# Order of steps in a float64-to-float32 weight conversion, and of GpSimd's block sums, in a fused attention and Fourier-MLP kernel

## The chip, the cores and the metric

The kernel runs on one core of one Trainium2 chip. The metric is the device time of one execution in microseconds (us). A core has five engines with a queue of instructions each: TensorE (PE in the profile, with its weight loads as PEld), VectorE (DVE), ScalarE (ACT), GpSimd (POOL) and SyncE (SP), which here issues most of the DMA transfers. An engine takes its own queue in order; between engines, an instruction waits for the instruction whose data or buffer it needs.

## The reference

Chunked attention gives x; a Fourier mixing and an MLP with layer norm follow:

```python
scores = scale * np.matmul(q_c, k_c.transpose(0, 1, 2, 4, 3))   # 8 batches, 8 heads, 9 chunks of 64, D 64
attn = np.exp(scores - max); attn = attn / (sum + 1e-09)
x = np.matmul(attn, v_c)                                        # bridged to (8, 576, 512)
u = x + np.real(fft(fft(x, axis=1), axis=2))
un = (u - mu) / np.sqrt(var + 1e-06)
out = u + np.maximum(un @ w_ch1, 0.0) @ w_ch2                   # w_ch1 512x2048, w_ch2 2048x512
```

The two weight matrices arrive as float64. VectorE and ScalarE have to turn every weight into float32 from its two 32-bit halves before TensorE can use it.

## The kernel before

The work goes through nine groups of token tiles (`groups`), each with an up product (`w1`), a Relu and a down product (`w2`). Group 0 runs plainly (`up_first`, then `down_plain`), group 1 has a plain up product and a down product in half-sized blocks, and the later groups use half-sized blocks for both, whose sums and differences of weight blocks are stored in device memory once (`keep1`, `keep2`, both on GpSimd). The code is under a manual schedule: the order of the calls in the Python program is the order in each engine's queue.

The main loop (lines 1315 to 1352) takes one step of `mlp(g)` at a time and counts it in `t`. Group 0 has KF = 16 up steps (`t` 1 to 16: four blocks `f` of four output tiles, four steps `kk` each) and 16 down steps (`t` 17 to 32: one row block m of `w2` each, four matmuls). On every fourth up step the block is complete and ScalarE writes four Relus (line 1065), which read the PSUM tiles that the next block needs. Behind each step of the MLP the body of the loop puts, in this order: the next steps of the attention and Fourier work of the next batch (`sides`: transposes, scores, softmax, `att_V`, folding, then `fourier`), then weight pieces (`round_next`), then up to three steps of the sums for `keep2` (line 1337).

**A weight piece.** There are 32 pieces of 128x512 weights: 0 to 15 are `w1`, 16 to 31 `w2`; down step m needs piece 16 + m. The raw halves land by DMA in one of seven spaces (`spaces`), from piece 26 on in three only; a piece's load can start once the piece before it in that space is read out. `round_weight(i)` puts the first half of piece i ("h") and then the second half of piece i - 1 ("t") into the queues:

- VectorE 322: fraction bits (AND), into the place of the weight; ScalarE 314: turned into a float between 1 and 2.
- VectorE 325: exponent bits (AND), into `power`; ScalarE 317 and 320: two Relus that make a power of two of them.
- for piece i - 1, VectorE 335: the low half is added to the fraction (waits for 314); 336: the sign is set on the power (waits for 320); 337: fraction times power. Line 341 then issues the next load.

The steps `t` = 1 to 16 call `round_next` five times in four steps (twice at `t` = 4, 8, 12), so pieces 7, 12, 17 and 22 are those begun at `t` = 3, 7, 11 and 15, the steps ahead of the Relus. Piece 0 is converted on its own in `attention_early`, ahead of the copies of `fourier_early` (lines 846 to 856), and the first half of piece 1 lies behind these (line 857, its ScalarE steps put off by hand).

**The joining.** `fourier(1)` sends its second products at `t` = 23 (`z_sets`, line 669). ScalarE copies four short rows (`z_middle`, 708) and two half tiles (`z_odd`, 694), VectorE joins them (`z_joined`, 699 and 703), ScalarE spreads the result (732 to 735 into `zr`, then `zf`), and TensorE can run the first mixing product (`mix`, 788). The rows `y` (793) are combined on VectorE (798, 799) and added to x by VectorE and, for the mirrored tiles, GpSimd (805); mean and variance (652, 653) and the normalized rows `un` (942) follow, which TensorE transposes (347) for group 1.

**The sums of `keep2`.** Each of four rounds has four GpSimd operations (line 1017), an operand of which is the `w2` that VectorE has finished, and seven stores. They write into spaces that raw pieces have used. `n_sum < 5` lets the first four sums and their stores in once piece 26 is begun, the others once all pieces are done.

Of the kernel before, what the change touches and what calls it, by code (L numbers as in the profile page):

```python
# [8 lines left out]
FP32 = mybir.dt.float32  # L9
U32 = mybir.dt.uint32  # L10
ACTF = mybir.ActivationFunctionType
ALU = mybir.AluOpType
# [4 lines left out]
def kernel(  # L17
# [32 lines left out]
    nc = tc.nc  # L50
# [10 lines left out]
    KF = DFF // 128  # L61
# [84 lines left out]
    N_LATE, N_EARLY, N_LAST = 5, 8, 26  # L146
# [108 lines left out]
    def load_tables():  # L255

        token_tables(early_tk)
        for i in range(2):
            nc.sync.dma_start(out=first_rest[32 + 32 * i:33 + 32 * i, 0:DM], in_=dim_tab[0:1, 1 + 2 * i, :])
# [10 lines left out]
    def turn_dim_tables():  # L270
# [9 lines left out]
    pieces = [  # L280
        (w1[:, kk, f:f + 512], w_ch1[kk * 128:(kk + 1) * 128, f:f + 512])
        for f in range(0, DFF, 512)
        for kk in range(KD)
    ] + [(w2[:, m, :], w_ch2[m * 128:(m + 1) * 128, :]) for m in range(KF)]

    power = {}
# [3 lines left out]
    def raw(i):  # L290
        return spaces[raws[i]].bitcast(U32).rearrange("p (f r) -> p f r", r=2)

    def load_weight(i):

        fit = [r for r in free if (i < N_EARLY or r < N_LATE) and (i < N_LAST or r > 1)]
        if i < len(pieces) and fit:
            raws[i] = fit[0]
            free.remove(fit[0])
            nc.sync.dma_start(out=raw(i).rearrange("p f r -> p (f r)"), in_=pieces[i][1].bitcast(U32))

    def round_weight(i, later=None, parts="ht"):

        if "h" in parts and i < len(pieces):
            w, t = pieces[i][0], raw(i)
            lo, hi, wi = t[:, :, 0], t[:, :, 1], w.bitcast(U32)  # L310
            p = power[i] = three_p.tile([128, 512], U32, tag="o", name="power")

            def fraction(w=w, wi=wi):
                nc.scalar.activation(out=w, in_=wi, func=ACTF.Copy, scale=2.0 ** -20, bias=1.0)

            def exponent(p=p):
                nc.scalar.activation(out=p, in_=p, func=ACTF.Relu, scale=-1.0, bias=top[:, 0:1])

            def power_(p=p):
                nc.scalar.activation(out=p, in_=p, func=ACTF.Relu, scale=-8.0, bias=top[:, 1:2])  # L320

            nc.vector.tensor_scalar(wi, hi, 0x000FFFFF, None, ALU.bitwise_and)
            if later is None:
                fraction()
            nc.vector.tensor_scalar(p, hi, 0x7FF00000, None, ALU.bitwise_and)
            if later is None:
                exponent()
                power_()
            else:
                later += [fraction, exponent, power_]  # L330
        if "t" in parts and 0 < i <= len(pieces):
            w, t = pieces[i - 1][0], raw(i - 1)
            lo, hi = t[:, :, 0], t[:, :, 1]
            p = power.pop(i - 1)
            nc.vector.scalar_tensor_tensor(w, lo, 2.0 ** -52, w, ALU.mult, ALU.add)
            nc.vector.scalar_tensor_tensor(p, hi, 0x80000000, p, ALU.bitwise_and, ALU.bitwise_or)
            nc.vector.tensor_tensor(out=w, in0=w, in1=p.bitcast(FP32), op=ALU.mult)
            r = raws.pop(i - 1)
            if i - 1 + len(spaces) < N_EARLY or r < N_LATE:
                free.append(r)  # L340
            load_weight(max(raws, default=i - 1) + 1)
# [694 lines left out]
    lo, hi = slice(0, 256), slice(256, 512)  # L1036
# [203 lines left out]
    with tc.manual_schedule():  # L1240
        nc.vector.memset(warm, 0.0)
        make_identity(nc, ident)
        nc.vector.memset(eps, 1e-6)
        for r in range(4):
            nc.vector.memset(sign[32 * r:32 * r + 32], 2.0 * (r % 2) - 1.0)
        nc.vector.memset(top[:, 0:1], float((896 + 255) << 20))
        nc.vector.memset(top[:, 1:2], float(255 << 23))
        nc.scalar.preload_act_table_set("natural_log_exp_and_others")
        first_rest = three_p.tile([128, XW], FP32, tag="y", name="first_rest")
        for t in more_v + v_ring:  # L1250
            nc.vector.memset(t[:, :, :, D:DV], 1.0)
        for n in range(first[1]):
            load(n)
            if n < 3:
                load_v(n)
        load_v(3)
        load_v(4)
        load_tables()
        load_weight(0)
        load_dim_tables()  # L1260
        for i in range(1, len(spaces)):
            load_weight(i)
        n_w = 2
        idle = [ps_f.tile([128, 512], FP32, tag="ff", name="idle")]
        early_xp = [ps_f.tile([128, 512], FP32, tag="ff", name="early_xp") for _ in range(2)], None

        def keep_warm(times):

            for _ in range(times):
                nc.tensor.matmul(out=idle[0][:, 0:NQ], lhsT=warm[:, 0:128], rhs=warm[:, 0:NQ], start=True, stop=True)  # L1270

        put_off, first_ups = [], []

        def round_next(later=None):
            nonlocal n_w
            if n_w <= len(pieces):
                round_weight(n_w, later)
                n_w += 1

        keep_warm(8)  # L1280
        attention_early()
        turn_dim_row()
        for step, _ in enumerate(fourier_early()):
            if step == 0:
                turn_dim_tables()
        round_next()
        PAUSE = 3

        def side(b):
            yield from attention(b)  # L1290
            for _ in range(PAUSE if b == 1 else PAUSE - 1):
                yield
            yield from fourier(b)

        sides = [list_ for list_ in (side(b) for b in range(1, B))]
        sizes = []
        for b in range(1, B):
            n_tiles = first[b + 1] - first[b]
            sizes.append((4 * n_tiles + 1 if b == 1 else 3 * n_tiles + 1) + PAUSE + 2 + (b == 1) + NM + b % 2)
        done, cur = 0, 0  # L1300
        begin = [0]
        for g in range(NG):
            begin.append(begin[-1] + (KF if g < first_of[1] else 2 * HF) + (KF if g < first_of[2] else 2 * NO))
        ready_at = [begin[g] + (2 * KF - 7 if g < first_of[2] else 2 * HF + 4) for g in range(NG)]
        conv2 = iter([step for i in range(HF // 2) for step in [keep2(i)]])
        conv1 = iter([step for i in range(4) for step in [keep1(i)]])

        def chain(gens):
            for gen in gens:
                yield from gen  # L1310

        n_sum = 0
        conv2, conv1 = chain(conv2), chain(conv1)
        t = 0
        for g in range(NG):
            for _ in mlp(g):
                t += 1
                heavy = False
                if t == 8:
                    nc.scalar.copy(tk, early_tk[:, :, :, 0:NE])  # L1320
                if cur < len(sides):
                    t0 = 3 if cur == 0 else ready_at[cur - 1]
                    t1 = ready_at[cur]
                    due = min(sizes[cur], (t - t0) * sizes[cur] // (t1 - t0))
                    while done < due:
                        heavy = next(sides[cur], None) or heavy
                        done += 1
                    if t >= t1:
                        for _ in sides[cur]:
                            pass  # L1330
                        cur, done = cur + 1, 0
                if not heavy:
                    round_next()
                    if t <= 2 or t < KF and t % 4 == 0 or t >= KF + 3:
                        round_next()

                for _ in range(3):
                    if n_w > len(pieces) or n_w > N_LAST and n_sum < 5:
                        next(conv2, None)
                        n_sum += 1  # L1340
                if t == begin[1] - 1:
                    for _ in conv2:
                        pass
                if begin[1] <= t < begin[1] + KF // 2:
                    for _ in range(3):
                        next(conv1, None)
                if t == begin[1] + KF // 2:
                    for _ in range(NS2):
                        fetch(2)
                if t == begin[1] + KF:  # L1350
                    for _ in range(NS1):
                        fetch(1)
# [49 lines left out]
```

## Time and profile before

| | us |
|---|---|
| median of 3 runs (lowest, highest) | 1082.01 (1081.83, 1082.57) |
| the profiled execution: its time, and its span from first to last instruction | 1083.94, 1082.2 |
| TensorE busy in matmuls, share of the span | 1057.6, 98% |
| VectorE, ScalarE, GpSimd busy | 586.8, 309.4, 328.6 |
| TensorE idle that another engine ends, from 50 to 200 us | 1.1 + 2.6 + 4.4 + 0.5 + 0.4 |

From 240 us on TensorE is busy without a gap in almost every stretch of 20 us (in two of them it is 1.8 and 0.8 us short) until the last stretch; the idle time lies before, in the stage in which the weights are converted. There VectorE is busy 18 to 19.7 us of every 20 from 40 to 140 us, ScalarE 16 to 18 of every 20 from 40 to 100 us.

How to read the lines of the profile: a wait line has the engine and line that waited, what ended the wait, then the total, the number of times and the longest in us. A line of the timeline has the start, the time in us, engine, line, operation, and the tile written <- the tiles read; in square brackets stands the idle time of the engine just before it. In the chain of waits, a line has the start, the time and the engine and line that the end of the program hung on at that moment. In the table by stretches, each engine has its busy time and count, then come the clock granted to TensorE (1.00 is full speed), the share of the DMA engines' time, and GB/s.

### The profile page before, as it was taken

The numbers are of one execution on the slowest core, as the hardware profiler recorded it, in microseconds if no ns is written. First come the engines' busy times: TensorE is split into PE (matmuls) and PEld (weight loads), VectorE is DVE, ScalarE is ACT, GpSimd is POOL, SyncE is SP. The second block draws the span as 40 slices with busy tenths as digits, with TensorE's granted clock in tenths as the row PEclk, the third lists the DMA queues.
The fourth block names the chain that finished last, engine by engine and source line by source line (L and its number), as shares of the span: only waits on it lengthen the run. The fifth ranks groups of instructions, "written<-read, shape, count | busy, mean of one in ns | idle before, by whom it ended". The sixth has DMA issues, their size and how long they took to land.

```text
span 1082.2 us, 19747 instructions
## 1 busy us (share of the span) xinstructions
PE 1057.6 (98%) x7410; PEld 841.1 (78%) x7410; DVE 586.8 (54%) x1271; ACT 309.4 (29%) x730; POOL 328.6 (30%) x475
## 2 busy tenths in 40 slices
PE   8999989999999999999999999999999999999998
PEld 6645445446888888788888888888888888888887
DVE  4899986325556555664555555735664534323411
ACT  4788463222113320232122311331134103101300
POOL 4301026384513350163215331525151401310140
PEclk9999989999999999999999999999999999999999
DMA  8766555598557635793578356854663355346232
GB/s 176 237 196 180 153 175 199 143 292 275 192 172 229 198 118 173 222 266 105 168 214 252 112 176 179 253 174 150 184 199 104 144 173 177 123 151 213 78 117 78
DMA packets 147948, 192.65 MB, mean 178 GB/s; under 512 B 66284, under 2 KB 104172, under 8 KB 140686
## 3 DMA queue, kind: packets, MB, share of 16 engines
q1 hardware_dynamic: 144204, 187.98, 57.1%
q10 hardware_dynamic: 3330, 2.76, 1.0%
q8 instruction: 59, 0.97, 0.3%
q0 software_dynamic: 320, 0.66, 0.3%
q14 instruction: 35, 0.29, 0.1%
HBM read 167.22 MB, written 24.12 MB: 177 GB/s over the span
## 4 chain that ended last, share of the span: by engine, by line
PE 81%; DVE 6%; DMA 6%; ACT 4%; SPq 2%; issue 1%; POOL 1%; DVEq 0%; ACTq 0%; POOLq 0%
PE pb L1190 21%; PE pa L1141 17%; PE pa L1190 15%; PE pb L1141 13%; PE pt L347 3%; PE up L1074 2%; PE dn L1095 2%; PE mix L788 2%; PE z L669 1%; PE sc L398 1%; PE xp L448 1%; PE up L1054 1%; DMA v<-in_v_dram 1%; DMA out_dram<-o 1%; DMA q<-in_q_dram 1%
## 5 line engine op out<-in xcount | busy, mean ns | idle before, releaser
L1141 PE MATMUL pa<-unT,wa 128*128 128x256 f32 x672 | 159.9, 381 | 2.5 <-DVE wa L1149 2.5
L1141 PEld LDWEIGHTS pa<-unT,wa 128*128 128x128 f32 x672 | 126.3, 190 | 20.3 <-DVE wa L1149 3.0
L1042 POOL TENSOR_TENSOR h<-h 128x256 f32<-128x256 f32 x64 | 55.2, 870 | 232.6 <-DVE wb L1040 140.1
L1190 PE MATMUL pa<-wb,h 128*128 128x256 f32 x512 | 115.7, 380 | 0.0
L1190 PE MATMUL pb<-wb,h 128*128 128x256 f32 x512 | 114.9, 379 | 0.0
L1141 PE MATMUL pb<-wa 128*128 128x256 f32 x448 | 106.6, 381 | 0.0
L1190 PEld LDWEIGHTS pa<-wb,h 128*128 128x128 f32 x512 | 96.1, 190 | 12.9
L1190 PEld LDWEIGHTS pb<-wb,h 128*128 128x128 f32 x512 | 96.3, 190 | 12.6
L1141 PEld LDWEIGHTS pb<-wa 128*128 128x128 f32 x448 | 84.3, 190 | 11.5
L1095 PE MATMUL dn<-wb,h 128*128 128x512 f32 x128 | 60.8, 625 | 2.6 <-ACT h L1065 2.6
L505 POOL COPY xall<-xall 1x512 f32<-1x512 f32 x28 | 17.3, 617 | 149.7 <-DVE xall L465 120.4
L1147 DVE TENSOR_TENSOR wa<-pb,wa 128x256 f32<-128x256 f32 x56 | 23.8, 424 | 69.7 <-ACT wa L1146 69.7
L1190 PE MATMUL pb<-wb,yall 128*128 128x256 f32 x256 | 58.2, 381 | 0.0
L1190 PE MATMUL pb<-wb 128*128 128x256 f32 x256 | 57.7, 379 | 0.0
L1190 PE MATMUL pa<-wb,yall 128*128 128x256 f32 x256 | 57.6, 379 | 0.0
L1074 PE MATMUL up<-unT,wa 128*128 128x512 f32 x128 | 56.8, 596 | 0.0
L1146 ACT COPY wa<-pa 128x256 f32<-128x256 f32 x56 | 20.8, 372 | 123.8 <-PE pa L1141 81.0
L1141 PE MATMUL pa<-wa 128*128 128x256 f32 x224 | 53.9, 383 | 0.0
L1141 PE MATMUL pb<-unT,wa 128*128 128x256 f32 x224 | 53.0, 380 | 0.0
L1190 PEld LDWEIGHTS pa<-wb,yall 128*128 128x128 f32 x256 | 48.0, 190 | 6.1
L1190 PEld LDWEIGHTS pb<-wb,yall 128*128 128x128 f32 x256 | 47.7, 190 | 6.3
L1190 PEld LDWEIGHTS pb<-wb 128*128 128x128 f32 x256 | 47.7, 190 | 5.9
(265 smaller groups left out, 1770.0 us busy)
## 6 DMA issues: line engine op xcount, KB each, us to landing
wb<-s SPq DMA_DIRECT2D x56, 1024.0 KB
wa<-s SPq DMA_DIRECT2D x196, 256.0 KB
xall<-in_moe_w_ch_dram SPq DMA_DIRECT2D x22, 512.0 KB
q<-in_q_dram SPq DMA_DIRECT2D x96, 112.0 KB
k<-in_k_dram SPq DMA_DIRECT2D x96, 112.0 KB
v<-in_v_dram SPq DMA_DIRECT2D x124, 64.0 KB
yall<-in_moe_w_ch_dram SPq DMA_DIRECT2D x10, 512.0 KB
s<-wb SPq DMA_DIRECT2D x20, 256.0 KB
```

The source lines that it names most:

```text
L347: nc.tensor.transpose(pt[:, j, :], src(j), ident)
L398: nc.tensor.matmul(out=sc[t0:t0 + CH, e, j * CH:(j + 1) * CH], lhsT=a[r0:r0 + D, 2 * j + c, 0:CH], rhs=b[r0:r0 + D, 2 * j + c, 0:CH], star ...
L448: nc.tensor.matmul(out=xp[0][e][t0:t0 + CH, j * DV:(j + 1) * DV], lhsT=a[r0:r0 + CH, j, t0:t0 + CH], rhs=b[r0:r0 + CH, c, j, :], start=Tru ...
L505: nc.gpsimd.tensor_copy(to, from_)
L788: nc.tensor.matmul(out=mix[:, cols], lhsT=zt[:, T], rhs=tab, start=(T == 0), stop=(T == 3), skip_group_check=True,)
L1042: nc.gpsimd.tensor_tensor(out=h1[:, m, hi], in0=h1[:, m, lo], in1=h1[:, m, hi], op=ALU.subtract)
L1074: nc.tensor.matmul(out=up, lhsT=w1[:, kk, m * 128:(m + 1) * 128], rhs=unT[:, kk], start=(kk == 0), stop=(kk == KD - 1),)
L1095: nc.tensor.matmul(out=dn, lhsT=h1[:, m, s * 128:(s + 1) * 128], rhs=w2[:, m, :], start=(m == 0), stop=(m == KF - 1),)
L1141: nc.tensor.matmul(out=dst, lhsT=w[:, kk, r], rhs=rhs[o][:, kk], start=(o in (0, 1) and kk == 0), stop=(kk == 1), skip_group_check=True,)
L1146: nc.scalar.copy(a, dst)
L1147: nc.vector.tensor_tensor(out=b, in0=pbs[r][:, 0], in1=a, op=ALU.add)
L1190: nc.tensor.matmul(out=dst, lhsT=lhs[:, m], rhs=w[:, m], start=(o in (0, 2) and m == 0), stop=(m == HF - 1), skip_group_check=True,)
```

## The change

Three edits:

1. In `round_weight`, VectorE's five steps come in another order: exponent bits of piece i, then 335 and 336 of piece i - 1, then the fraction bits of piece i, then 337 of piece i - 1. ScalarE's steps follow: the two Relus first (317, 320), the fraction (314) last. This holds for pieces 0 and 1 too.
2. The sums for `keep2` are put into the queue from `t` = KF + 7 = 23 on, as long as not all pieces are done.
3. Of the pieces begun at `t` = 3, 7, 11 and 15, the three ScalarE steps are put into the queue only at the beginning of the next step's body, which is behind the Relus and ahead of all else in that body.

```diff
+        head, tail = "h" in parts and i < len(pieces), "t" in parts and 0 < i <= len(pieces)
+        if head:
...
-            nc.vector.tensor_scalar(wi, hi, 0x000FFFFF, None, ALU.bitwise_and)
-            if later is None:
-                fraction()
             nc.vector.tensor_scalar(p, hi, 0x7FF00000, None, ALU.bitwise_and)
             if later is None:
                 exponent()
                 power_()
+        if tail:
+            w_, t_ = pieces[i - 1][0], raw(i - 1)
+            p_ = power.pop(i - 1)
+            nc.vector.scalar_tensor_tensor(w_, t_[:, :, 0], 2.0 ** -52, w_, ALU.mult, ALU.add)
+            nc.vector.scalar_tensor_tensor(p_, t_[:, :, 1], 0x80000000, p_, ALU.bitwise_and, ALU.bitwise_or)
+        if head:
+            nc.vector.tensor_scalar(wi, hi, 0x000FFFFF, None, ALU.bitwise_and)
+            if later is None:
+                fraction()
             else:
                 later += [fraction, exponent, power_]
...
+        if tail:
+            nc.vector.tensor_tensor(out=w_, in0=w_, in1=p_.bitcast(FP32), op=ALU.mult)
...
-        n_sum = 0
+        n_sum, late = 0, []
...
+                for do in late:
+                    do()
+                late = []
...
-                    round_next()
+                    round_next(late if t < KF and t % 4 == 3 else None)
...
-                    if n_w > len(pieces) or n_w > N_LAST and n_sum < 5:
+                    if n_w > len(pieces) or n_w > N_LAST and n_sum < 5 and t >= KF + 7:
```

In the built program, the queues of TensorE hold the same instructions in the same order as before. On GpSimd the order is the same up to the fifth sum; then both additions of line 805 come before the sixth, seventh and eighth sum, where two sums stood ahead of them, and one copy (368) comes two sums earlier. On SyncE, one set of four loads of `k` comes ahead of the second set of stores of `keep2`.

More of the change, by code (lines that the diff above doesn't have):

```diff
@@ L301, in round_weight @@
     def round_weight(i, later=None, parts="ht"):
-        if "h" in parts and i < len(pieces):
+        head, tail = "h" in parts and i < len(pieces), "t" in parts and 0 < i <= len(pieces)
+        if head:
             w, t = pieces[i][0], raw(i)
-            lo, hi, wi = t[:, :, 0], t[:, :, 1], w.bitcast(U32)
+            hi, wi = t[:, :, 1], w.bitcast(U32)
             p = power[i] = three_p.tile([128, 512], U32, tag="o", name="power")
@@ L328, in round_weight @@
                 power_()
+        if tail:
[7 more added lines that the diff above has]
+                fraction()
             else:
                 later += [fraction, exponent, power_]
[L331 to L337, printed above, removed]
+        if tail:
+            nc.vector.tensor_tensor(out=w_, in0=w_, in1=p_.bitcast(FP32), op=ALU.mult)
             r = raws.pop(i - 1)
```

## The prediction

> **What bounds the kernel now.** First I read what TensorE waited for, and the clock by stretches. The columns of the waits are total, times and longest, in us.
>
> ```profile
> PE mix L788 <- ACT zr L735: 4.4, 1, 4.4
> PE dn L1095 <- ACT h L1065: 2.6, 1, 2.6
> PE up L1054 <- ACT h L1065: 1.1, 2, 0.6
> ```
>
> ```profile
> 112.00:116.00 4.00, 2.62 (x37) 1.13 (x35) 4.00 (x7) 1.69 (x4) 0.00 (x0) 1.00 0.89 281
> 116.00:120.00 4.00, 2.81 (x4) 1.26 (x5) 3.42 (x10) 2.59 (x5) 0.22 (x2) 0.65 1.02 234
> ...
> 156.00:160.00 4.00, 3.83 (x10) 2.80 (x11) 2.91 (x7) 3.94 (x12) 0.00 (x0) 0.50 1.05 383
> ```
>
> TensorE is 98% busy, so only its gaps can be won. Three kinds concern the change: the Relus of the up product come late (0.64 us at 64.0, 0.44 at 97.5, 2.57 at 114.6), and the first mixing product waits 4.42 us for the joining (151.75 to 156.17). Each long gap brings slow clock behind it (0.65, 0.50). From 240 us on TensorE is full, so what is won at 177 us, where the joining's chain last hands over to TensorE, should reach the end.
>
> Next, the timeline of VectorE: the cycle of one piece, then the place where VectorE last waits for TensorE.
>
> ```profile
> 58.09 0.42 DVE L322 TENSOR_SCALAR wa<-xall 128x512 uint32<-128x512 uint32 x1
> 58.43 0.42 DVE L325 TENSOR_SCALAR power<-xall 128x512 uint32<-128x512 uint32 x1
> 58.77 0.68 DVE L335 SCALAR_TENSOR_TENSOR wa<-xall,wa 128x512 f32<-128x512 uint32 x1
> 59.37 0.68 DVE L336 SCALAR_TENSOR_TENSOR power<-xall,power 128x512 uint32<-128x512 uint32 x1
> 60.08 0.69 DVE L337 TENSOR_TENSOR wa<-wa,power 128x512 f32<-128x512 f32 x1
> 60.69 0.42 DVE L322 TENSOR_SCALAR wa<-yall 128x512 uint32<-128x512 uint32 x1
> ...
> 127.19 0.17 DVE L470 TENSOR_SCALAR rd<-xp 128x8 f32<-128x8 f32 x1 [1.14 <-PE xp L448]
> ```
>
> A cycle is 2.60 us from start to start: 0.34 + 0.34 + 0.60 + 0.71 + 0.61. Step 337 starts 0.1 us later behind 336 than 336 behind 335: it needs 336's result. And at 127.19 VectorE had only 1.14 us to spare: from there to the joining the chain of waits hangs on VectorE and two loads of raw weights.
>
> ```profile
> 137.00 3.64 DMA xall<-in_moe_w_ch_dram
> 140.66 1.33 DVE wb L322
> 141.99 1.41 DVE power L325
> 143.41 1.68 DVE wb L335
> ...
> 145.71 3.51 DMA xall<-in_moe_w_ch_dram
> ...
> 150.98 0.72 ACT power L320
> 151.71 0.10 ACT warm L708
> ```
>
> So if TensorE comes earlier at 114.6, this chain does not: it stands only 1.14 us behind it.
>
> **What the Trainium skill says.** "TensorE: Matmul & The Clock Gate", Part 1: an idle window of about 3.4 us halves TensorE's clock, and a busy one restores it. The trace agrees on the cost, not on the threshold: behind a gap of 2.57 us eight matmul records took 5.39 us where 3.44 is usual. The same page, on queue depths, calls ScalarE and VectorE strict FIFO; so it looks here: the Relus ran at 116.56, behind a piece's three steps that waited for VectorE. "SBUF — State Buffer", Terms: VectorE and GpSimd take one port pair by a lock, and the loser waits for the other's whole instruction; beside sums of 1.26 to 1.45 us, step 322 took 1.33 us for 0.42. "VectorE: DVE Perf Modes", on the DRAIN, says a semaphore between two operations costs nothing extra; here the dependent pair shows about 0.1 us more.
>
> **The change, part by part.** Starts are walked forward from the trace with its own start-to-start times: VectorE as above; ScalarE fraction 0.53, first Relu of the pair 0.74, second 0.63; 0.46 from a VectorE AND to ScalarE; 0.67 from the fraction's start to 335; 0.73 from 320 to 336.
>
> (a) *Order on VectorE.* Between 336 and 337 now lies the fraction's AND, which hides the dependence: 0.34 + 0.60 + 0.61 + 0.34 + 0.60 = 2.49, 0.11 less. But the AND starts 1.54 into the cycle and ScalarE makes the fraction last: 1.54 + 0.46 + 0.67 = 2.67, and 335 wants it at 2.49 + 0.34 = 2.83. Only 0.16 us is left, where before it was over 2 us. Whenever ScalarE is crowded, 335 waits, with four VectorE steps behind it, where before 336 waited with one.
>
> (b) *Piece 0.* Before, 314 at 33.77, 320 at 35.05, 336 at 35.80, 337 at 36.53, copy 848 at 37.19. After: 317 at 33.77, 320 at 34.51, 314 at 35.14, so 335 at 35.81, 336 at 36.41, 337 at 37.14, 848 at 37.79. Nothing hides these 0.60 us: 848 began as the products it copies ended, and the chain runs on from it (854, 856, the copies into zr, the norm). The MLP starts 0.60 later.
>
> (c) *Relus ahead of the late piece.* At 64 us they come as TensorE needs them: -0.64. But the late piece's 1.90 us then stand ahead of the copies 377 and 386, and the scores wait for the second: +0.44. With (b), TensorE is at +0.40 - 0.40 = about 0 at 67 us. At 97.5: -0.44, which the scores at 106 may give back (they need 472 read out). At 114.6 the Relus no longer stand behind the piece that came at 114.20: dn starts by about 114.4, some 2.8 us earlier, without the 1.95 us of slow clock. TensorE is then 4 to 5 us ahead at 118.
>
> (d) *VectorE until then.* It is level at 79.8, where it waited 0.83 for the scores. From there ten pieces give -1.1, and the old wait of 0.67 at 101.5 goes. New waits of 335 or 336 for ScalarE: 1.1 at 85, where the Relus, the late piece, the copy 1320 and an exponential run together, and 0.4, 0.75 and 1.0 around 98 to 103. Sum: -1.1 - 0.67 + 3.25 = +1.5; I take +1.1, since some of it is hidden where ScalarE drains. So VectorE is free at 126.05 + 1.1 = 127.15, and 470 starts there: gain 0.05, for all that TensorE is ahead. The ends: no new waits (126.05 - 1.8, gain 2.9), or all of them twice (+4.7, loss 3.6).
>
> (e) *Pieces 24 to 29, 132.4 to 151.6.* Step 336 of piece 24 comes at 3.42 in place of 3.88, so the load it frees lands 0.46 earlier; the same for the next load, plus 0.6, since the two slowed steps behind it count less; the fraction of piece 29 then ends at 18.4 behind 132.4, where 320 ended at 19.2. Gain 0.8. The cover of (c) is gone here: TensorE waits at the mix some 8 us in place of 4.4.
>
> (f) *Sums.* The new condition holds no sum back: in the built queue nothing stands between the old and the new place, and the second sum waits for the 337 of piece 25 in both. So the 3.0 us lost at 140.7 to 145 (1.33 + 1.49 + 1.75 in place of 0.42 + 0.42 + 0.69) stay. What moves is behind the joining: sums 6 and 7 no longer run beside and ahead of 805, which took 1.32 for 0.69 and on GpSimd began 0.3 late: -0.9 together. Against it, ScalarE's fractions of pieces 30 and 31 stand ahead of `y` and come last: +0.46; the fifth sum may block 337: 0 to +0.5. Net -0.2. Sums 6 to 8 end about 1.1 us later; GpSimd waited 5.3 us behind them (to 191.4), which hides it. On SyncE the loads of k go four issues earlier, and the stores behind sum 8 wait 1.1 longer: nothing on the path, by that same slack; at worst +0.5.
>
> Sum: 0.05 + 0.8 + 0.2 = 1.05, call it -1.1. TensorE's longer idle at the mix adds no more than the spread of re-warming, ±0.5 (5.4 us at half speed now). Against the profiled execution: span 1082.2 - 1.1 = 1081.1, with the 1.7 around it 1082.8 for its 1083.94. That execution lies 0.18% above the median, so I take the difference from the median: 1082.0 - 1.1 = 1080.9.
>
> **Rivals.** *VectorE's shorter cycle comes through* (no new waits, d's good end in half): for it, ScalarE is busy only 65% to 91% of the stage (20 us stretches); against it, the 0.67 waits behind Relus. 470 gains 1.3: 1082.0 - 1.3 - 0.8 - 0.2 = 1079.7. *ScalarE's crowd decides* (slower): at each block of Relus the fraction, last in its row, holds 335, place 98 to 127 us. It decides once VectorE comes more than 1.14 + 1.0 = 2.1 us late at 126.05; three more waits of 1.0 make +4.1: 470 loses 3.0, 1082.0 + 3.0 - 1.0 = 1084.0. For it: the slack of 0.16. *The sums do leave the joining*, as edit 2 says: another 3.0 off, 1077.9; against it the queue's waits. *All of the gap at 114.6 comes through*: 2.8 + 1.9 + 0.2 = 4.9, 1077.1; against it the 1.14.
>
> **How the numbers follow.** Measurement of this kernel can tell about 0.2% (2.2 us) from no change. Forecast 0.47 (1080.0 to 1082.0), shorter cycle 0.27 (1078.3 to 1080.3), crowd 0.14, sums 0.07, whole gap 0.05. Below 1079.85: half of the second, the last two, a little of the first: 0.29. Above 1084.2: half of the third: 0.08. The range leaves out the two fast cases' low half and the worse half of the crowd: 1077.9 to 1083.6.
>
> **What would show it.** Right: dn (1095) starts at about 114.4 at full clock; 335 with waits for 314 in the middle of the stage; 470 within 1 us of 127; the wait for zr grows from 4.4 to 7 to 9 us; sums still beside 140 to 145; 848 0.6 later. Wrong: no 335 waits and 470 before 126; or slow steps gone at 140; or the mix later than 156.2.

## The result, and the profile after

The changed kernel takes 1088.12 us, median of 7 runs (1086.67 to 1089.66), against 1083.78 us for the kernel before in 7 runs made with them (1081.83 to 1086.03). The ratio is 1.0040 (95% interval 1.0025 to 1.0056): 4.3 us slower. The forecast was 1.1 us faster. (The three runs shown above for the kernel before had a median of 1082.01.) The profiled execution of the changed kernel took 1086.67 us (span 1084.9), the lowest of its seven.

TensorE's longest waits after 112 us, changed kernel (lines are 3 higher than before behind `round_weight`; total, times, longest):

```profile
PE sc L401 <- DVE rd L464: 5.8, 1, 5.8
PE z L682 <- ACT warm L759: 3.5, 1, 3.5
PE mix L791 <- DVE y L802: 2.1, 1, 2.1
PE mix L791 <- ACT zr L738: 1.0, 1, 1.0
```

The wait for a Relu at 114.6 is gone. The wait of 4.4 us at the mixing product has given way to three shorter ones (6.6 us in all), and there is a wait of 5.8 us for the scores that the forecast doesn't have. The clock by stretches, same kernel:

```profile
112.00:116.00 4.00, 4.00 (x41) 1.88 (x40) 4.00 (x8) 3.18 (x6) 0.00 (x0) 1.00 0.81 244
116.00:120.00 4.00, 4.00 (x14) 2.02 (x13) 3.49 (x9) 2.44 (x4) 0.22 (x2) 1.00 0.89 224
...
220.00:224.00 4.00, 3.79 (x36) 2.23 (x37) 2.52 (x8) 0.00 (x0) 2.83 (x3) 0.53 0.91 292
```

Between 112 and 120 TensorE is now full and at full clock, where it had been 0.65 at the end. At 220 it runs at half clock, behind the new wait. VectorE's timeline, same kernel: one cycle, the read-out of the attention, one of the slow steps beside the sums:

```profile
56.24 0.41 DVE L323 TENSOR_SCALAR power<-xall 128x512 uint32<-128x512 uint32 x1
...
57.18 0.67 DVE L331 SCALAR_TENSOR_TENSOR power<-xall,power 128x512 uint32<-128x512 uint32 x1
57.78 0.41 DVE L333 TENSOR_SCALAR wa<-xall 128x512 uint32<-128x512 uint32 x1
58.11 0.67 DVE L339 TENSOR_TENSOR wa<-wa,power 128x512 f32<-128x512 f32 x1
58.72 0.41 DVE L323 TENSOR_SCALAR power<-xall 128x512 uint32<-128x512 uint32 x1
...
126.56 0.16 DVE L473 TENSOR_SCALAR rd<-xp 128x8 f32<-128x8 f32 x1
...
140.92 1.75 DVE L330 SCALAR_TENSOR_TENSOR wb<-xall,wb 128x512 f32<-128x512 uint32 x1
```

The cycle is 2.48 us, the read-out comes at 126.56 in place of 127.19, and the sums still run beside VectorE's steps at 141. Starts in us, from the timelines, for the two kernels and for the four experiments that take the change apart:

| | before | after | no_late_sums | late_sums_alone | order_alone | late_relus_alone |
|---|---|---|---|---|---|---|
| `dn`, first down product | 117.19 | 114.10 | 115.11 | 116.77 | 119.33 | 113.12 |
| `mix`, first mixing product | 156.17 | 154.77 | 156.02 | 155.78 | 157.39 | 154.70 |
| `pt` <- `un`, behind the joining | 177.45 | 176.29 | 177.96 | 176.64 | 179.23 | 175.97 |
| loads of `k` behind the outputs, SyncE | 206.20 | 209.72 | 206.79 | 209.78 | 208.02 | 205.50 |
| scores of these `k` | 217.01 | 220.21 | 217.28 | 219.66 | 218.74 | 215.35 |
| next transposition, 24 matmuls on | 228.04 | 232.89 | 228.31 | 232.30 | 229.77 | 226.38 |

At 177 the profiled execution stands 1.16 us ahead, near what was forecast, and at 210 still (209.76 against 210.92, the transposition ahead of the scores). By 233 it is 4.85 us behind: the scores start 3.20 later than before, and the matmuls up to the next transposition take 12.68 us in place of 11.03. The chain of waits of the changed kernel (start, time, what) shows the place:

```profile
203.49 8.43 DMA out_dram<-o
211.93 0.34 SPq L203
212.31 0.43 SPq L203
212.79 6.16 DMA k<-in_k_dram
219.07 1.09 DVE kT L369
220.21 1.13 PE sc L401 x32
```

The scores wait for the read-out 464, which stands on VectorE behind the transposition of `k` (369), which waits for the load of `k`. In the kernel before, the same load was asked for 3.5 us earlier.

SyncE's queue says why. Its waits for output stores from 180 to 212 us, first the kernel before, then the changed one:

```profile
SPq L226 <- DMA out_dram<-o: 2.6, 1, 2.6
SPq L203 <- DMA out_dram<-o: 1.8, 1, 1.8
SPq L1003 <- DMA out_dram<-o: 1.6, 1, 1.6
```

```profile
SPq L1024 <- DMA out_dram<-o: 4.8, 1, 4.8
SPq L203 <- DMA out_dram<-o: 2.0, 2, 1.8
SPq L226 <- DMA out_dram<-o: 1.5, 1, 1.5
```

And its timeline, changed kernel:

```profile
185.00 1.80 SPq L203 DMA_DIRECT2D k<-in_k_dram  x4
...
190.07 5.53 SPq L1024 DMA_DIRECT2D s<-wb  x2
195.70 0.41 SPq L1024 DMA_DIRECT2D s<-xall  x1
196.21 4.42 SPq L226 DMA_DIRECT2D v<-in_v_dram  x4
```

The two stores at 190.07 belong to the last of `keep2`'s four sets of seven. They store `w2` itself (`wb`), so no sum is waited for: their data was there. But in the built program nearly every transfer issued by SyncE or ScalarE waits for the one eight before it in their common program order: the program uses eight completion counters in turn for these two engines (GpSimd has others), and a counter is used again only when the transfer that used it last is done. By edit 2 the loads of `k` come ahead of this fourth set of stores (the fourth, not the second), and the set now falls among ScalarE's four stores of the first output tiles. The second of the two stores has the first of these output stores eight places ahead, and that can't start before 193.57, when VectorE has made the tile. SyncE stands still until about 195.2, with this store, one more, four loads of `v`, four of `q`, eight output stores and the loads of `k` behind it. In the kernel before it was the last load of `v` and loads of `q` that met ScalarE's output stores (the 2.6 us above), and less was left behind them.

### The profile page after: what moved, and what is told of

Read it like the earlier page. It is cut to its first block, busy times and chain, and to the rows that moved or that the text cites. A ratio compares the mean times of both kernels' runs of the same rounds, so it can differ in the third digit from the quotient of the medians.

```text
span 1084.9 us, 19749 instructions
## 1 busy us (share of the span) xinstructions
PE 1057.8 (98%) x7410; PEld 841.4 (78%) x7410; DVE 585.3 (54%) x1271; ACT 310.7 (29%) x730; POOL 329.8 (30%) x475
## 4 chain that ended last, share of the span: by engine, by line
PE 84%; DVE 6%; DMA 4%; ACT 3%; issue 2%; SPq 1%; POOL 0%; ACTq 0%; DVEq 0%; POOLq 0%
PE pb L1193 20%; PE pa L1144 18%; PE pa L1193 15%; PE pb L1144 13%; PE up L1077 4%; PE pt L350 3%; PE mix L791 2%; PE sc L401 1%; PE xp L451 1%; PE z L672 1%; PE dn L1098 1%; DMA xall<-in_moe_w_ch_dram 1%; PE up L1057 1%; DVE power L331 1%; DMA v<-in_v_dram 1%
```

## The experiments

Theories: **A**, the loss is this place in SyncE's order; **B**, the new order on VectorE and ScalarE pushes a transfer to a bad place; **C**, the sums end too late (187.4 in place of 186.1) and the stores wait for them; **D**, the order of transfers itself costs, not the wait. Times are medians, with the ratio to the kernel before on the same chip (95% interval); the differences in us are worked out from these ratios.

**no_late_sums**: the changed kernel with the diff's last edit undone.

```diff
-                    if n_w > len(pieces) or n_w > N_LAST and n_sum < 5 and t >= KF + 7:
+                    if n_w > len(pieces) or n_w > N_LAST and n_sum < 5:
```

> The changed kernel with GpSimd's sums let go as before (the condition on the step taken out again); the order on VectorE and ScalarE stays changed. Theory A, the loss comes from the sums' later place in the program, which puts the stores of the last sums on SyncE behind ScalarE's four output stores: 1.1 to 2 us below the kernel before, and TensorE's wait of 5.8 us in the scores at 220 is back to 1.4 or less. Rival B, the new order on VectorE and ScalarE moves some transfer into a bad place: 3 to 4.5 us above the kernel before, with the wait of 5.8 us.

1083.42 against 1083.44 us, ratio 1.0000 (0.9988 to 1.0013). The wait of 5.8 us is gone (two of 2.0 in all remain), so the slowdown is edit 2's. But no gain of 1.1 to 2 us shows either: edits 1 and 3 together bring nothing that can be measured (the interval is -1.3 to +1.4 us).

**late_sums_alone**: the kernel before with only that edit.

> The kernel before with nothing but the condition on GpSimd's sums. SyncE's order of transfers is then that of the changed kernel to the last one. Theory A: 3 to 5 us above the kernel before, a wait of 4 us or more of a store on SyncE for an output store of ScalarE near 190, and TensorE waits some 5 us in the scores near 217. Rival B: within 1 us of the kernel before.

1087.20 us, ratio 1.0045 (1.0031 to 1.0058), +4.9. A store on SyncE waits 5.6 us for an output store, TensorE 4.9 us for the scores. A holds, B falls.

**sums_catch_up**: the changed kernel with the sums' place restored from `t` = 25 on.

```diff
-                for _ in range(3):
+                for _ in range(4 if KF + 8 <= t <= KF + 9 else 3):
```

> The changed kernel, but four steps of the sums instead of three in the two steps of the MLP after the first that may have sums, so that from there on the program has the sums and their stores where the kernel before has them. GpSimd still begins late, and its last sum should still end about 1.2 us later than before. Theory A (the place of the stores in SyncE's order decides): 0 to 1.5 us below the kernel before, no store on SyncE waits over 1 us for an output store. Rival C (the sums themselves end too late, and the stores wait for them): 2 to 4.5 us above the kernel before. Rival B: 3 to 4.5 above.

1084.74 us, ratio 1.0016 (1.0005 to 1.0027), +1.7: far below the changed kernel, but a miss for A's 0 to -1.5. No store of `keep2` waits for an output store. But SyncE comes to its own output stores at 200.56, 0.75 later than in no_late_sums, `k` is transposed 0.73 later (216.87 against 216.14), and TensorE waits 1.83 us for the scores where no_late_sums has 1.2. In the profiled execution the matmuls behind this wait also met slow clock and took 12.73 us in place of 11.03 (see the hardware). Whether the other executions met it there is not shown.

**only_tail_late**: the kernel before, with only the later sums delayed.

```diff
-                for _ in range(3):
+                for _ in range(2 if KF + 8 <= t <= KF + 9 else 3):
```

> The kernel before, but two steps of the sums instead of three in the two steps of the MLP from the 24th: the first sums go as before, on GpSimd the sums hardly move (its queue is full to the end anyway), but the stores of the last sum come behind the loads of k and among ScalarE's output stores in SyncE's order, as in the changed kernel. Theory A: 3 to 5 us above the kernel before, the wait in the scores near 217 is 4.5 us or more. Rival C: within 1 us of the kernel before, since the sums end where they ended. Rival B: within 1 us.

1086.50 us, ratio 1.0036 (1.0020 to 1.0051), +3.9; the scores wait 3.85 us (4.5 or more was expected). Here the loads of `v` behind the stores wait 4.3 us for the output stores. The first sums are where they were and the last ends at 186.6, so C falls: what moves the stores behind the loads of `k` is enough.

**after_outputs_on_gpsimd**, **before_outputs_on_gpsimd**: the four output stores issued by GpSimd, in the changed kernel and in the one before.

```diff
-                    eng = nc.scalar if r else nc.sync
+                    eng = (nc.gpsimd if n in groups[0] else nc.scalar) if r else nc.sync
```

> The changed kernel, but the four output stores of the first group of tiles that ScalarE issued are issued by GpSimd, so that no transfer of SyncE comes to wait for them; SyncE's own order stays that of the changed kernel. Theory A, the form of it in which the wait for those stores is the cause: no store on SyncE waits for an output store near 190, the loads of k for the next tiles start 4 us or more earlier than 209.7, TensorE's wait of 5.8 us at 220 is gone; 0 to 3 us below the kernel before. Rival D (the order of the transfers by itself, so many of them ahead of the loads of k, is the cause): 2 to 4.5 us above. A risk for A: GpSimd waits with its next sums until the outputs are there, some 5 us.

1081.21 us, ratio 0.9978 (0.9970 to 0.9987), -2.4. SyncE's order is that of the changed kernel, and its timeline is now:

```profile
189.32 1.55 SPq L1024 DMA_DIRECT2D s<-wb  x2
...
191.56 2.85 SPq L226 DMA_DIRECT2D v<-in_v_dram  x4
...
203.27 3.47 SPq L203 DMA_DIRECT2D k<-in_k_dram  x4
```

The two stores take 1.55 us in place of 5.53, the loads of `k` start 6.45 us earlier, the scores don't wait. D falls: it was the wait. The last sum ends as late as in the changed kernel (187.5), which speaks against C once more. GpSimd's next sums begin at 196.66 in place of 190.38, which shows in no wait of TensorE.

> The kernel before with the same four output stores issued by GpSimd. Theory A: the waits of 2.6 and 1.8 us for output stores on SyncE between 190 and 199 go, and with them TensorE's wait of 1.4 us in the scores at 217: 0.5 to 2 us below the kernel before. Rival D: within 0.5 us of it.

1081.43 us, ratio 0.9982 (0.9973 to 0.9991), -2.0: the kernel before lost some of the same at this place.

**order_alone** (edit 1), **late_relus_alone** (edit 3): the diff of the change, cut to that edit.

> Only the other order of a piece's steps on VectorE; ScalarE's parts and GpSimd's sums as in the kernel before. SyncE's order of transfers is that of the kernel before. The forecast's reckoning (cycle of a piece 2.49 us, gain held back by the wait for the scores): 0.5 below to 0.2 us below the kernel before. Rival (the fraction stands last on ScalarE and VectorE waits for it, and the copy of one element that TensorE's mid products wait for stands behind a held fraction): 0.3 to 1.5 us above.

1085.59 us, ratio 1.0024 (1.0015 to 1.0034), +2.6: the rival's side, and more. VectorE waits 7.7 us for fractions up to 130 us (0.4 in the kernel before, which waited 2.0 for powers). ScalarE, then VectorE, at one of the two longest of these waits:

```profile
64.95 1.09 ACT L1068 ACTIVATE h<-up 128x512 f32<-128x512 f32 x2
65.91 0.61 ACT L380 COPY qT<-pt 128x512 f32<-128x512 f32 x1
66.37 0.63 ACT L389 COPY kT<-pt 128x512 f32<-128x512 f32 x1
...
68.28 0.61 ACT L315 ACTIVATE wa<-wa 128x512 f32<-128x512 uint32 x1
```

```profile
68.93 0.69 DVE L330 SCALAR_TENSOR_TENSOR wa<-yall,wa 128x512 f32<-128x512 uint32 x1 [2.09 <-ACT wa L315]
```

Four Relus, two copies, exponent and power stand ahead of the fraction, and VectorE waits 2.09 us, with four steps behind the waiting one.

> Only ScalarE's part of every fourth piece behind the Relus of the next step; VectorE's order and the sums as in the kernel before. The forecast's reckoning: the products into the output begin about 2.6 us earlier than 117.2, without the wait for a Relu, but the joining is reached no more than 0.5 us earlier: 0.6 below to 0.2 us below the kernel before. Rival (all of it comes through): 2 to 2.6 us below. Rival (nothing comes through, since what is gained at 117 is waited away before the joining, and a new wait behind the joining is added): 0 to 0.7 us above.

1082.29 us, ratio 0.9989 (0.9976 to 1.0003), -1.2, with an interval that reaches from -2.6 to +0.3: between the reckoning and the rival in which all comes through, and not clear of no change. In the profiled execution the down products begin at 113.12, 4.1 earlier than before, the mixing product 1.5 earlier (0.5 at most was reckoned), and that stays to 226.

**fraction_first**, **fraction_second**, **fraction_in_the_middle**: other orders on VectorE in the kernel before, to find what in edit 1 costs. "A" is the AND for the fraction, "E" that for the exponent, 335 to 337 the steps of the piece before; each AND's ScalarE part follows it.

```
before                  A E 335 336 337      new order               E 335 336 A 337
fraction_first          A 335 336 E 337      fraction_second         E A 335 336 337
fraction_in_the_middle  E 335 A 336 337
```

> The new order of a piece on VectorE with its two AND steps exchanged: the AND for the fraction first, then the two steps of the piece before, the AND for the exponent between them and the product. ScalarE then has the fraction first again, exponent and power last. Nothing else differs from the kernel before. Theory E (the order alone costs 2.6 us because VectorE waits for the fraction, which stands last on ScalarE behind Relus and copies: 7.7 us of waits up to 130): the waits for the fraction shrink below 2 us, the cycle is still 2.49 us, and the time is between 1.5 us below and 0.5 us above the kernel before; a wait of the last AND-OR step for the power, up to 3 us in all, may take part of it. Rival F (any order with the exponent's part late makes VectorE wait just as long, now for the power): 1.5 to 3 us above.

1087.89 us, ratio 1.0042 (1.0032 to 1.0051), +4.5: theory E's numbers are missed, the rival's exceeded. VectorE waits 3.3 us for fractions and 2.7 for powers, the cycle is 2.575 us. An AND that comes late on VectorE also holds ScalarE's queue with the Relus in it: TensorE waited 6.8 us for `h` in place of 3.7.

> The kernel before with the two AND steps of a piece exchanged, nothing between them: the AND for the exponent first, then that for the fraction, then the three steps of the piece before. On ScalarE the fraction stands last, as in the changed kernel, but from the start of its AND to the step that reads the fraction there are 2.9 us on VectorE (3.3 in the kernel before, 1.3 in the new order). Theory G (what costs is the lead that ScalarE has, not its order of steps): waits for the fraction below 2 us up to 130, cycle 2.60, 0.3 us below to 0.8 us above the kernel before. Rival H (the fraction's last place on ScalarE is what costs): 1.8 to 3 us above.

1085.80 us, ratio 1.0017 (1.0006 to 1.0027), +1.8; 5.0 us of waits for fractions.

> The kernel before with the AND for the fraction moved between the two AND-OR steps of the piece before, so that the lead is 2.0 us and the dependent pair of the last two steps stays (cycle 2.60 us). Theory G: waits for the fraction between those of the kernel before and of the new order alone (0.4 and 7.7 us up to 130), 0.8 to 2.2 us above the kernel before. Rival H: as the new order alone or worse for the longer cycle, 2.4 to 4 us above. If the lead doesn't matter: within 0.5 us.

1087.33 us, ratio 1.0034 (1.0023 to 1.0045), +3.7; 6.6 us of waits. H's times came in both (the first at its edge), G's in neither. But the waits are not H's alone: the last place on ScalarE with the lead nearly as before brings 5.0 us, and they grow as the lead gets shorter.

| from the start of the fraction's AND to its reader, us | 3.3 (before) | 2.9 (second) | 2.0 (middle) | 1.3 (new order) |
|---|---|---|---|---|
| VectorE's waits for ScalarE's part up to 130, us | 2.4 | 5.0 | 6.6 | 7.7 |
| cycle, us | 2.60 | 2.60 | 2.60 | 2.49 |
| time against before, us | 0 | +1.8 | +3.7 | +2.6 |

An estimate from these figures: some 22 cycles up to 126 us give 22 x 0.11 = 2.4 us back in the new order; with the waits of the kernel before that makes 7.7 - 2.4 - 2.4 = 2.9 us of loss, near the 2.6 measured. fraction_first, with 6.0 us of waits, costs more than this sum; its longer waits for `h` go that way, but they were not tried alone.

**late_sums_outputs_on_gpsimd**, **late_relus_outputs_on_gpsimd**, **late_relus_sums_outputs**: the kernel before with the output stores on GpSimd and edit 2, edit 3, or both.

> The kernel before with the condition on the sums and with the four output stores on GpSimd. Theory A: without the wait for these stores the later sums cost nothing and their own gain behind the joining shows, 0.4 us as the traces have it from the products of the joining to the transposition at 177: 1.8 to 3 us below the kernel before, that is 0 to 1 us below the one with the stores on GpSimd alone. Rival D (the order of the transfers costs by itself): 0.5 us below to 2 us above the kernel before.

1081.26 us, ratio 0.9975 (0.9966 to 0.9985), -2.7 against the -2.0 of the stores alone: without the wait, edit 2 shows no cost.

> The kernel before with ScalarE's part of every fourth piece behind the Relus and the four output stores on GpSimd. If the two gains add (1.2 and 2.0 us): 2.6 to 3.8 us below the kernel before. If the earlier begin of the products is waited away elsewhere (GpSimd's next sums, the weights): 1.5 to 2.5 below.

1079.93 us, ratio 0.9962 (0.9950 to 0.9975), -4.1: the two gains (-1.2 and -2.0) add, within the interval.

> The same with the condition on the sums too, so all of the change but VectorE's new order, with the stores out of SyncE's way. If the three gains add (1.2, 0.4 and 2.0 us): 3 to 4.5 us below the kernel before. Rival D: the sums cost 1 us or more against the kernel without them.

1079.41 us, ratio 0.9962 (0.9948 to 0.9976), -4.1. A third gain can't be told from none, so the last two kernels are equally the best found. This kernel is after_outputs_on_gpsimd without edit 1, and that one gained 2.4: edit 1 costs some 1.7 us here too, though the two intervals overlap a little.

## Why the prediction was wrong

**Step (f) failed**: "On SyncE the loads of k go four issues earlier, and the stores behind sum 8 wait 1.1 longer: nothing on the path, by that same slack; at worst +0.5." The order was known from the built program, but the only wait that was reckoned for a store was that for its sum, and the slack was GpSimd's. The stores waited 4.8 us for something else, an output store of ScalarE, and SyncE's queue has no such slack: the loads of `k` at its end set the scores at 220. In place of at worst +0.5 stands +4.9 (late_sums_alone). That is the whole of the miss in sign: without edit 2 the two kernels take the same time, to within some 1.4 us.

The rest of (f): the sums do stay at 140 to 145, as reckoned. From `mix` to `pt` <- `un` the later sums gain 0.42 us (21.52 against 21.94 in no_late_sums, 20.86 against 21.28 without the other edits) where 0.9 was put down. At the start of `un` on ScalarE they gain 0.81 without the other edits (19.61 against 20.42), so the reckoning was near; but TensorE, still at its products there, began `pt` later than `un` allowed, and the rest of the gain is lost. With the other edits they gain 0.30 (20.66 against 20.96). Edit 1 takes 0.66 from `mix` to `pt` (21.94 against 21.28), where 0.46 was put down: `y` waits behind step 339, and no_late_sums also has slow clock there.

**(a)**: the cycle is 2.49, as walked. The 0.16 us that were "left" were too little: edit 1 by itself is +2.6, and the rival in which ScalarE's crowd decides, which had 0.14, names its cause. In the changed kernel edit 3 takes part of the crowd away, and VectorE waits 5.2 us for fractions.

**(b)** is right: VectorE's copies start 0.28 later, at 37.47, although TensorE's products ended 0.39 earlier there.

**(c)** is right on `dn`: 114.10 (by about 114.4 was said), at full clock.

**(d)** is right too, and the experiments show both of its sides. The executions don't all start alike: in no_late_sums VectorE waits 0.98 us for the first raw weights. So the stretch from the first AND (32.94 us in the changed kernel, 33.32 before) to the read-out says more than the time of 126.56 by itself (127.15 was forecast):

| first AND to read-out, us | before | after | no_late_sums | order_alone | late_relus_alone |
|---|---|---|---|---|---|
| | 93.87 | 93.62 | 93.85 | 96.26 | 91.75 |

Edit 3 alone brings 2.1 us to this point and edit 1 alone takes 2.4; together 0.25 and 0.02 are gained, where 0.05 was said.

**(e)**: TensorE does wait longer ahead of the mix, 3.5 + 2.8 us in no_late_sums against 4.4; 7 to 9 was said. The first part, for a copy of one element (759) that stands on ScalarE behind a held fraction, was not seen; what it costs by itself was not tried. From the first AND the mix is 1.02 earlier in the changed kernel and 0.51 in no_late_sums; 0.05 + 0.8 was said.

So the -1.16 at 177 agrees with the forecast's sum partly by chance: 0.38 of it is the earlier start of that execution, and no_late_sums, from its first AND, is 0.15 behind at 177, with slow clock on the way. Without edit 2 the median shows 0.0. Alone, edit 3 gives -1.2 and edit 1 +2.6; together they would be +1.4. That they are less may be because edit 3 spares VectorE some of its waits for fractions (5.6 us in no_late_sums in place of 7.7). ScalarE's part of the four late pieces, and of piece 1, also has the fraction first and not last (315 at 63.18 us, 318 at 63.71, 321 at 64.45 in the changed kernel).

That the changed median is 4.3 above and the profile only 2.7: of the 4.85 us at 228, TensorE's last waits for converted blocks (`pa` <- `wa`) give 1.6 back (2.5 to 0.9), and the profiled execution is the lowest of its seven.

## What to carry to other kernels

When a change moves instructions in program order, walk every transfer that moves through its issuing queue, and ask of each not only when its data is ready but what else it waits for: a transfer can wait for an unrelated earlier one, of another engine too, and all that is queued behind it waits along. A dependent pair's small stall on one engine is cheap against the lead that another engine needs: an AND moved down by three steps saved 0.11 us a cycle and brought 5.3 us more of waits. Price a reorder with no reserve as a loss where the other engine's queue is shared with work for a third.

## What the runs showed of the hardware

*The same wait can bring slow clock or not.* From the start of the scores to the next transposition, the same matmuls took 11.03 us behind waits of 1.2 us (no_late_sums), 1.43 (before) and 1.77 (fraction_first), but 12.73 behind 1.83 (sums_catch_up), 12.51 behind 3.85 (only_tail_late), 12.64 behind 4.95 (late_sums_alone) and 12.68 behind 5.79 (after). In sums_catch_up:

```profile
218.01 0.69 PE L401 MATMUL sc<-kT,qT 64*64 64x64 f32 x32 [1.83 <-DVE rd L464]
```

```profile
220.00:224.00 4.00, 4.00 (x7) 1.51 (x6) 0.42 (x1) 0.00 (x0) 3.92 (x4) 0.63 0.61 169
```

So where slow clock comes here it costs 1.5 to 1.7 us, and 4 us more of waiting add none. But the length of the wait doesn't settle whether it comes. The first down products behind the same wait of 2.57 us, up to 120 us, in the kernel before and in only_tail_late:

```profile
117.19 3.67 PE L1095 MATMUL dn<-wb,h 128*128 128x512 f32 x4 [2.57 <-ACT h L1065]
```

```profile
117.56 2.84 PE L1095 MATMUL dn<-wb,h 128*128 128x512 f32 x6 [2.57 <-ACT h L1065]
```

Four take 3.67 us in the one and six take 2.84 in the other, which runs at full clock; the eight up to the next transposition take 5.22 and 3.54. In the same way 2.05 us ahead of a mixing product brought slow clock in no_late_sums and 2.08 us at the same place none in the changed kernel. Of TensorE's waits of 0.9 us or more between 40 and 260 us in all traces, none up to 1.77 us brought slow clock and each of 3.19 us or more did; between these it went both ways (still none behind 2.80 us at the first mixing product of no_late_sums). What decides there is not shown. So the 1.95 us of slow clock that the prediction read behind the gap at 114.6 need not come in every execution. "TensorE: Matmul & The Clock Gate", Part 1, in the Trainium skill, has idle windows of about 3.4 us for this; here slow clock came behind waits of 1.83 us and more.

*Which engine issues a store can matter.* "DMA: Bandwidth & Descriptors", Rules for kernel authors, in the Trainium skill, says that spreading transfers over the issuing engines doesn't help bandwidth and only saves issue time. Four stores moved from ScalarE to GpSimd took 2.0 us off the kernel before and about 6.7 us off the changed one (ratios 1.0040 and 0.9978 to the kernel before), though not by bandwidth: SyncE no longer waited for them, since in this program GpSimd's transfers don't share the counters of the other two.
